# The last expert's kept sums in a fused attention and mixture-of-experts kernel: additions by engines in place of accumulating transfers, a last batch by eight products, and input quarters made earlier

## The chip, the cores and the metric

The kernel runs on one core of one Trainium2 chip. The metric is the device time of one execution in microseconds (us). In the main comparison the four executions of the kernel before lie within 0.3% (832.15 to 834.22 us). The kernel before took a median of 832.4 us in the main comparison. Experiments are compared by their ratio to runs of the kernel before on the same chip. A profiled execution has a span, from the first to the last instruction, that is 1.7 to 1.9 us shorter than its device time.

Engines: PE is TensorE (matrix products), PEld its weight loads, DVE is VectorE, ACT is ScalarE, POOL is GpSimd, SP is SyncE, which here only issues transfers. Sixteen DMA engines move the data. A transfer issued by POOL appears in a software queue (q0) of the profile, one issued by SP or ACT in a hardware queue (q1, q10).

## The reference, cut to what matters

```python
# attention with a hash mask: B, H, S, D = 4, 8, 768, 64; its output becomes x: 3072 tokens x 512
logits = x @ w_gate                      # 8 experts; P: 8 rounds of row and column normalisation
out = np.zeros((N, D), dtype=np.float32)
for e in range(E):                       # w1[e]: 512 x 1024, w2[e]: 1024 x 512
    h = np.maximum(x @ w1[e], 0.0)
    ye = h @ w2[e]
    out += P[:, e:e + 1] * ye
```

Every expert works on every token. The sum over the experts is what the change is about.

## The kernel before

The kernel keeps the whole output, 3072 x 512 in f32, as running sums `acc` in SBUF, and adds each expert to it. For experts 1 to 7 both products use a scheme with seven products of half-size blocks in place of eight, paid for with sums of the blocks ("quarters" of x, w1 and w2, and the half sums `hs` of h). Per expert there are four batches of 768 tokens. While TensorE makes the hidden layer of one batch (`hidden`), it makes the second product of the batch before (`mixed`) in between: `woven` interleaves the two step by step.

One step `i` of `mixed` makes two blocks of 128 tokens. Of its products three are gathered straight into `acc` by VectorE, and four intermediate ones are copied, scaled, to a tile `vt` by ScalarE. The copies are then added to `acc` by an accumulating transfer:

```python
    outv = out.rearrange("(b r j m) d -> b j m r d", b=B, r=R, j=J)
    # ... cut: in mixed(e, b), for each i; vt is [128, 4, 256] f32, 512 KB
            def keep(k, p):
                if last and k == 1:
                    gather(k, a, p)
                    return
                pin(nc.scalar.activation(out=vt[:, k], in_=a, func=Act.Copy, scale=p))
                # ... cut: in the very last step VectorE adds vt[:, k] itself
            # ... cut: the seven products
                if g == 6:
                    if not last:
                        pin(nc.gpsimd.dma_start(out=acc[:, b, i], in_=vt, accum_op=Alu.add))
                    if e == E - 1 and not last:
                        for j in (i, J // 2 + i):
                            pin((nc.gpsimd if final else nc.sync).dma_start(
                                out=outv[b, j], in_=sums_of(b, j).rearrange("p c d -> p (c d)")))
                    next(coming)          # one step of GpSimd's work on the next expert's weights
```

With the last expert each pair of blocks is stored as soon as its transfer has landed: 22 stores of 256 KB, and for the very last pair four of 128 KB. Look at the order in `outv`: for fixed `b, j` a store's target is `m r d`, that is 4 x 32 x 512, because a tile's partition is `m * 32 + r` while neighbouring rows of the output differ in `m`.

The quarters of x are made by VectorE, one batch per round of the weave, in the first three rounds:

```python
        parts = quarters_of_x(n + 1) if n + 1 < B else iter(())
        # ...
            if g in (10, 19, 28, 37):
                next(parts, None)         # one of four VectorE operations, 128 x 768 f16
```

GpSimd makes the quarters of the next expert's weights at the same time, one operation of 128 x 1024 f16 after each accumulating transfer that it issues.

The softmax here doesn't subtract the row's maximum and nothing guards it: scores larger than these inputs give would overflow.

## Time and profile before

| | before |
|---|---|
| time, median of 3 runs | 832.17 us (832.15 to 834.22) |
| span of the profiled execution | 832.5 us |
| TensorE's last product ends | about 791.6 us |
| TensorE busy from 345 to 778 us | 432.66 of 433 us |
| TensorE idle from 270 to 320 us | 5.15 us |

First the page's picture of the span in 40 slices of 20.8 us, busy tenths of TensorE and of the DMA engines, kernel before.

```profile
PE   3979999999899899999999999999999999999800
DMA  6965687531020454666496467648745864456743
```

TensorE works until slice 38 and does nothing in the last two. The DMA engines still do. The second view gives the busy time of each engine by stretch: us of the stretch, then busy us and instructions of each engine, the granted clock of TensorE, the DMA share and GB/s.

```profile
270.00:320.00 50.00, 44.85 (x326) 31.45 (x324) 44.84 (x87) 36.28 (x81) 15.39 (x12) 1.00 0.49 85
320.00:345.00 25.00, 24.45 (x183) 17.66 (x182) 17.70 (x42) 19.86 (x44) 10.61 (x8) 1.00 0.45 86
345.00:778.00 433.00, 432.66 (x3278) 319.94 (x3277) 330.07 (x772) 282.82 (x657) 162.61 (x130) 1.00 0.63 115
```

From 345 us to the tail TensorE is the limit and has no gap worth speaking of. Between 270 and 320 us it idles 50 - 44.85 = 5.15 us.

The chain of waits, kernel before, its end: start in us, duration, what was waited for.

```profile
783.90 10.41 DMA acc<-vt
794.32 1.22 issue
795.53 0.53 POOL out_dram L288
...
796.97 21.15 DMA acc<-vt
818.12 0.28 issue
818.40 0.71 POOL out_dram L288
```

Two accumulating transfers, one after the other, take 31.6 of the last 48.6 us. Over the whole run such a transfer takes a median of 4.9 us. The timeline of the store queue and the DMA queues say why these take longer. The two first lines are issues of single stores by SP, one early and one late; the third, from the table of DMA queues for 794 to 796 us, when only stores were moving, gives packets, MB and share of 16 engines.

```profile
758.41 0.54 SPq L288 DMA_DIRECT2D out_dram<-acc  x1
805.13 5.16 SPq L288 DMA_DIRECT2D out_dram<-acc  x1
q1 hardware_dynamic: 98, 0.20, 26.6%
```

An issue takes 0.54 us when the queue has room and 5.16 us when it must wait for room. Stores alone move 0.20 MB in 2 us, about 100 GB/s, and keep 26.6% of the 16 engines busy: 0.266 x 16 = 4.3, as if four engines were at their limit and twelve had nothing to do. The Trainium skill, "DMA: Bandwidth & Descriptors", section "Why a DMA increments its semaphore by 16 and not by 1", says that a transfer is spread over the largest number of engines, up to 16, that divides the slowest dimension of both sides. Here that is 4, from 4 x 32 x 512 in DRAM.

Last, the timeline of 278 to 291 us, lines of GpSimd's and VectorE's additions alone.

```profile
279.22 2.45 POOL L139 TENSOR_TENSOR s<-t 128x1024 f16<-128x1024 f16 x1
279.38 2.73 DVE L646 TENSOR_TENSOR xT<-xT 128x768 f16<-128x768 f16 x1
...
285.20 0.55 DVE L648 TENSOR_TENSOR xd<-xT 128x768 f16<-128x768 f16 x1
...
287.68 2.97 DVE L650 TENSOR_TENSOR xd<-xT,xd 128x768 f16<-128x768 f16 x1
287.82 2.41 POOL L141 TENSOR_TENSOR t<-t 128x1024 f16<-128x1024 f16 x1
```

An operation of this form on VectorE takes 0.55 us alone. The two here that run beside one of GpSimd take 2.7 and 3.0 us, and they end 0.4 us after GpSimd's. The skill, "SBUF — State Buffer", section "Who interferes with whom", describes a port pair that such two operations share and that one of them holds for the whole instruction.

### The profile page before, as it was taken

How to read it: one execution, taken by the hardware profiler on the slowest of the kernel's cores; microseconds unless marked ns; L12 is line 12 of the kernel's file. 1: busy time of each engine (PE TensorE's matmuls, PEld its weight loads, DVE VectorE, ACT ScalarE, POOL GpSimd, SP SyncE). 2: the span in 40 equal slices, each digit the busy share in tenths (PEclk: the TensorE clock that was granted, in tenths of full speed). 3: DMA queues.
4: the chain of work that ended last, by engine and by line, in shares of the span. 5: the costliest groups of instructions: out<-in, count | busy, mean ns of one | idle time of the engine just before them, and what ended most of it. 6: DMA issues, size and time to landing. Idle time of an engine off the chain costs nothing.

```text
span 832.5 us, 16856 instructions
## 1 busy us (share of the span) xinstructions
PE 755.4 (91%) x6412; PEld 525.8 (63%) x6412; DVE 540.0 (65%) x1213; ACT 515.1 (62%) x1033; POOL 309.2 (37%) x323
## 2 busy tenths in 40 slices
PE   3979999999899899999999999999999999999800
PEld 1546656666555666677777777777777777777600
DVE  3435645654566897777777777777777777777700
ACT  0758767678645767766666666666666666666400
POOL 7655245439000333443353344334534433311110
PEclk9879999999899999999999999999999999999965
DMA  6965687531020454666496467648745864456743
GB/s 168 271 158 154 123 200 182 136 78 29 1 51 2 76 95 83 109 126 122 77 162 118 76 119 135 115 90 144 125 87 101 148 108 89 89 106 138 145 112 83
DMA packets 44912, 94.33 MB, mean 113 GB/s; under 512 B 10848, under 2 KB 24160, under 8 KB 44832
## 3 DMA queue, kind: packets, MB, share of 16 engines
q0 software_dynamic: 30112, 77.88, 48.7%
q1 hardware_dynamic: 13920, 14.77, 6.5%
q8 instruction: 50, 0.82, 0.4%
q10 hardware_dynamic: 800, 0.62, 0.3%
q14 instruction: 30, 0.25, 0.1%
HBM read 53.14 MB, written 7.08 MB: 72 GB/s over the span
## 4 chain that ended last, share of the span: by engine, by line
PE 75%; DMA 10%; ACT 5%; DVE 2%; issue 2%; POOL 2%; SPq 1%; POOLq 0%; ACTq 0%; DVEq 0%
PE a L663 17%; PE a L240 16%; PE d L663 12%; PE y L240 8%; PE st L458 5%; DMA acc<-vt 4%; PE d L240 4%; PE hp L516 4%; PE yp L198 2%; PE num L474 2%; ACT pt L461 2%; DMA qs<-t 2%; PE yp L526 2%; PE hp L306 2%; ACT acc L231 2%
## 5 line engine op out<-in xcount | busy, mean ns | idle before, releaser
L247 ACT ACTIVATE vt<-a,p 128x256 f32<-128x256 f32 x335 | 158.8, 474 | 154.6 <-PE a L240 154.6
L672 DVE CUSTOM_DVE_ANT_0 hT<-d,u 128x384 f16<-128x384 f32 x336 | 185.2, 552 | 98.9 <-ACT u L668 95.8
L285 POOL DMA_DIRECT2D acc<-vt x83 | 71.5, 861 | 324.1 <-ACT vt L247 146.8
L461 ACT ACTIVATE pt<-st 128x768 f16<-128x768 f32 x192 | 147.2, 809 | 71.5 <-PE st L458 50.5
L668 ACT COPY u<-a 128x384 f32<-128x384 f32 x336 | 161.2, 480 | 26.6 <-PE a L663 21.1
L240 PEld LDWEIGHTS <-hT 128*128 128x128 f16 x1344 | 131.0, 97 | 52.5 <-issue 2.2
L240 PE MATMUL a<-t,hs 128*128 128x256 f16 x1008 | 151.2, 272 | 4.4 <-ACT vt L247 3.2
L240 PEld LDWEIGHTS <-hs 128*128 128x128 f16 x1008 | 98.4, 98 | 41.8 <-issue 6.0
L663 PEld LDWEIGHTS <-t 128*128 128x128 f16 x896 | 87.7, 98 | 39.1 <-issue 2.9
L458 PE MATMUL st<-qs,ks 71*128 71x384 f16 x384 | 97.7, 337 | 16.2 <-DMA qs<-ds 11.9
L663 PE MATMUL d<-xd,t 128*128 128x384 f16 x448 | 109.4, 326 | 2.6 <-DVE hT L672 2.6
L663 PE MATMUL a<-xT,s 128*128 128x384 f16 x448 | 109.4, 326 | 0.1
L240 PE MATMUL y<-t,hT 128*128 128x256 f16 x672 | 100.7, 272 | 1.2 <-DVE acc L254 1.0
L254 DVE SCALAR_TENSOR_TENSOR acc<-y,p,acc 128x256 f32<-128x256 f32 x168 | 80.2, 478 | 11.7 <-PE y L240 11.6
L474 PEld LDWEIGHTS <-pt 128*128 128x128 f16 x1152 | 62.5, 99 | 28.2 <-issue 3.4
L663 PEld LDWEIGHTS <-s 128*128 128x128 f16 x672 | 65.5, 97 | 17.6 <-issue 2.3
L474 PE MATMUL num<-va,pt 128*128 128x65 f16 x1152 | 68.4, 196 | 0.6 <-ACT pt L461 0.6
L370 POOL CAST t<-acc 128x768 f16<-128x768 f32 x32 | 26.4, 828 | 89.0 <-DVE acc L369 88.2
L458 PEld LDWEIGHTS <-ks 71*128 71x128 f16 x384 | 33.3, 100 | 37.2 <-issue 14.3
L702 ACT ACTIVATE hT<-a 128x384 f16<-128x384 f32 x112 | 54.1, 483 | 1.8 <-PE a L663 1.7
L663 PE MATMUL a<-xd,s 128*128 128x384 f16 x224 | 54.3, 323 | 0.8 <-ACT u L668 0.6
L663 PE MATMUL a<-xT,t 128*128 128x384 f16 x224 | 54.7, 326 | 0.0
(94 smaller groups left out, 965.5 us busy)
## 6 DMA issues: line engine op xcount, KB each, us to landing
acc<-vt POOLq DMA_DIRECT2D x83, 512.0 KB, 4.9
t<-in_moe_w_dram POOLq DMA_DIRECT2D x24, 512.0 KB, 7.6
acc<-in_k_dram POOLq DMA_DIRECT2D x7, 768.0 KB, 5.8
acc<-in_q_dram POOLq DMA_DIRECT2D x7, 768.0 KB, 6.4
v<-in_v_dram POOLq DMA_DIRECT2D x28, 192.0 KB, 4.7
out_dram<-acc SPq DMA_DIRECT2D x18, 256.0 KB
t<-in_moe_w_dram POOLq DMA_DIRECT2D x4, 1024.0 KB, 10.6
ks<-t SPq DMA_DIRECT2D x64, 48.0 KB
```

The source lines that it names most:

```text
L240: pin(nc.tensor.matmul(dst, hq[hn][:, fo, :], wq[wn][:, fo, :], start=first and fo == 0, stop=fo == FH - 1, skip_group_check=True))
L247: pin(nc.scalar.activation(out=vt[:, k], in_=a, func=Act.Copy, scale=p))
L254: pin(nc.vector.scalar_tensor_tensor(out=dst, in0=src, scalar=p, in1=dst, op0=Alu.mult, op1=Alu.add))
L285: pin(nc.gpsimd.dma_start(out=acc[:, b, i], in_=vt, accum_op=Alu.add))
L458: pin(nc.tensor.matmul(st[:, i, 0:HT], d["k"][0:KR, h, kt * P:(kt + 1) * P], d["q"][0:KR, h, i * HT:(i + 1) * HT], start=True, stop=True))
L461: pin(nc.scalar.activation(out=pt, in_=st[:, :, 0:HT], func=Act.Exp, scale=scale))
L474: pin(nc.tensor.matmul(num[:, j * (D + 1):(j + 1) * (D + 1)], pf[:, j * P:(j + 1) * P], va[:, h, kt, :], start=(kt == 0 and j == 0), stop= ...
L516: pin(nc.tensor.matmul(hp[:, 0:HT], w1[:, do, fo * P:(fo + 1) * P], xT[:, do, b * S + t * HT:b * S + (t + 1) * HT], start=(do == 0), stop= ...
L663: pin(nc.tensor.matmul(bk, wq[wn][:, do, f * P:(f + 1) * P], xq[xn][:, do, :], start=first and do == 0, stop=do == 1, skip_group_check=True))
L668: pin(nc.scalar.copy(t, bk))
L672: pin(add(TENSOR_ADD_SAT, out=dst, in0=bk, in1=u, s0=3e38, s1=0.0))
L702: pin(nc.scalar.activation(out=hT[:, f, hi], in_=a, func=Act.Relu))
```

## The change

Its intent: no accumulating transfer with the last expert, so that the last stores don't wait for one; a last batch whose blocks are finished one after the other; and quarters of x that are all made before the second round.

```diff
@@ mixed
-                    if not last:
+                    if e < E - 1:
                         pin(nc.gpsimd.dma_start(out=acc[:, b, i], in_=vt, accum_op=Alu.add))
-                    if e == E - 1 and not last:
+                    else:
+                        eng = nc.vector if i == J // 2 - 1 else nc.gpsimd
+                        pin(eng.tensor_tensor(acc[:, b, i], acc[:, b, i], vt, op=Alu.add))
                         for j in (i, J // 2 + i):
-                            pin((nc.gpsimd if final else nc.sync).dma_start(
-                                out=outv[b, j], in_=sums_of(b, j).rearrange("p c d -> p (c d)")))
+                            pin(nc.sync.dma_start(out=outv[b, j],
+                                                  in_=sums_of(b, j).rearrange("p c d -> p (c d)")))
@@ new: the last batch of the last expert, by whole products
+    def final():
+        e, b = E - 1, B - 1
+        w2, hT = weights[e, 2], hts[e, b]
+        for j in range(J):
+            yp = (yps if j % 3 < 2 else y2ps).tile([P, DD], F32, tag="y", name="yp")
+            # ... cut: 8 products of 512 columns (the last block in two halves), then
+                pin(nc.vector.scalar_tensor_tensor(out=dst[:, cols], in0=yp[:, cols], scalar=...,
+                                                   in1=dst[:, cols], op0=Alu.mult, op1=Alu.add))
+                pin((nc.sync if cols.start == 0 else nc.scalar).dma_start(out=outv[b, j][:, :, cols],
+                                                                          in_=dst[:, cols]))
@@ woven
-        parts = quarters_of_x(n + 1) if n + 1 < B else iter(())
+        parts = chain(*(quarters_of_x(m) for m in range(1, B))) if n == 0 else iter(())
-            if g in (10, 19, 28, 37):
+            if g % 4 == 2:
                 next(parts, None)
```

Cut: for the last expert one sum of w2's blocks goes to a tile of its own instead of overwriting a quarter of w2, because `final` needs w2 as it was; `quarters_of_x` got a `yield` at its end; the special cases of the very last step fell away.

## The prediction

> **What bounds it now.** Up to 778 us TensorE: the busy table by stretch has it busy 432.7 of 433 us from 345 to 778, at full clock. Two places lose time.
>
> (1) The tail. The last product ends near 791.6 us, the span at 832.5. In between, the chain of waits holds almost only the last accumulating transfers `acc<-vt` (10.4 and 21.2 us; the median is 4.9) and the stores behind them. The store queue's timeline shows issues of 0.55 us until 760, then back-pressure of 4 to 7 us each. By the DMA view, stores alone (794 to 800) take 25.7% of 16 engines, 97 packets of 2 KB per 2 us, 97 GB/s: four busy engines, 85 ns a packet. The Trainium skill, "DMA: Bandwidth & Descriptors", section "Why a DMA increments its semaphore by 16 and not by 1", says a transfer is spread over the largest k up to 16 that divides both sides' slowest dimension; in DRAM the store's is 4 (4x32x512). The trace agrees. The accumulates need the same four engines and crawl.
>
> (2) From 270 to 320 TensorE idles 5.15 of 50 us (0.55 in the next 25). Four VectorE operations that make input quarters took 2.6 to 3.0 us instead of 0.55, each overlapping a 2.4 us GpSimd operation. The skill, "SBUF — State Buffer", section "Who interferes with whom", gives such a pair one exclusive port; the durations agree.
>
> **What changes.** Gone: 11 accumulating transfers, all of the last expert's. New: six GpSimd additions of 128x1024 f32 (estimate 2.4 us, as its f16 operations of 1024 columns), three on VectorE (estimate 1.2 us, from 422 ns at 256 columns). The last batch takes 48 products of 512 columns, 10.3 us, 1.71 a block, in place of 84 of 256 with stalls (13 us). Stores still have four engines. Eight quarter operations move to 250–270 us, where GpSimd does no arithmetic and VectorE is about half busy.
>
> **On the critical path.** Quarters: about 3.3 us back. VectorE's additions: up to 1 us lost. TensorE then ends near 788, and its own tail would end near 793. But stores bound the end: 128 packets on four engines are about 2.62 us a store. The third batch's middle pair, ready at 773, flows from 775 to 780, its last pair to 785.5, the last batch's six (five of 2.62, one in half rows, 3.2) to 802; completion and end add 2. So 804 us: some 3 us from the quarters, 25 from the tail.
>
> **Predicted: 804 us, 8 in 10 between 797 and 812. Faster by over 2%: 0.96; within 2%: 0.03; slower: 0.01.**
>
> **What would show it.**
> - No `acc<-vt` in the last expert; only hardware queues there, at 25% of 16 engines at the end.
> - Store issues of 0.55 us until about 775, back-pressure again for the last batch.
> - The last product ends 10 to 15 us before the last store lands; the chain ends in `out_dram<-acc`, not in TensorE.
> - TensorE's idle time from 270 to 320 falls below 2.5 us; no quarter operation takes over 1 us.
> - VectorE's half sums stay at 415 to 428 ns: GpSimd's additions end before they start.
>
> **What would make it wrong.** Stores on more than four engines: then the end is TensorE's, near 793. GpSimd additions over 4.5 us: they block half sums, and TensorE stalls six times by some us. Stores alone below 97 GB/s: 810 or later. The earlier quarters may delay the routing's VectorE chain at 250 to 256, under 1 us.

## The result, and the profile after

| | before | after |
|---|---|---|
| time, median of 4 runs | 832.44 us | 805.37 us (803.74 to 806.08) |
| ratio | 1 | 0.9668 (95% interval 0.9647 to 0.9688) |
| span of the profiled execution | 832.5 us | 804.0 us |
| VectorE's last operation, on TensorE's last product, ends | 792.2 us | 787.7 us |
| from there to the end of the span | 40.3 us | 16.3 us |
| TensorE idle from 270 to 320 us | 5.15 us | 1.52 us |

A ratio here is the mean time of one kernel's runs over that of the other's in the same rounds, so it is not quite the ratio of the medians.

The 40 slices, kernel after (20.1 us each).

```profile
PE   3969999999999999999999999999999999999991
DMA  6966676641002264486468657745964676541222
```

TensorE now works up to the last slice but one and a little into the last. The DMA share of the last three slices is a steady two tenths. Busy time by stretch, kernel after:

```profile
270.00:320.00 50.00, 48.48 (x358) 34.65 (x356) 35.97 (x85) 39.87 (x89) 17.99 (x14) 1.00 0.51 90
320.00:345.00 25.00, 24.26 (x181) 17.35 (x180) 18.21 (x43) 19.92 (x45) 9.33 (x9) 1.00 0.51 96
```

TensorE's idle time from 270 to 320 us fell from 5.15 to 1.52 us, and VectorE's busy time from 44.84 to 35.97 us. VectorE lost eight operations to an earlier stretch (8 x 0.55 = 4.4 us) and some 9 us that those had taken longer than 0.55 us beside GpSimd; part of the room is filled by other work that now comes sooner.

The chain of waits, kernel after, its end, followed by what SP, which waits for the last stores, waited for (total us, times, longest):

```profile
777.42 8.18 PE yp L304 x41
...
786.16 1.05 PE yp L304 x8
787.21 0.03 issue
787.24 0.48 DVE acc L306
```

```profile
SPq L796 <- DMA out_dram<-acc: 9.0, 5, 2.5
```

The chain view stops at VectorE's last operation at 787.7 us, because it goes back from the last instruction and the landing of a store is none. The 16.3 us that follow are the stores. The lines of the store queue show them: two groups of issues (line 290 is in `mixed`, line 309 in `final`; durations are ns, lowest, median and highest), then the DMA queue between 796 and 800 us.

```profile
L290 SPq DMA_DIRECT2D out_dram<-acc x18: 536/537/633, 727.6 to 777.6; - x18
L309 SPq DMA_DIRECT2D out_dram<-acc x6: 537/1466/4467, 778.7 to 790.1; - x6
q1 hardware_dynamic: 205, 0.41, 26.3%
```

The 18 stores of the first three batches issue without any wait. The six of the last batch come every 1.7 us and are held back up to 4.5 us, and after TensorE has ended, the queue still empties at 0.41 MB in 4 us, again on a quarter of the engines.

What the change added was cheap, as this view of groups by shape shows (line, engine, operation, count, busy us, mean ns):

```profile
L288 POOL TENSOR_TENSOR acc<-acc,vt 128x1024 f32<-128x1024 f32 x6 | 14.1, 2357 | 38.8 <-DVE acc L254 30.4 <-ACT vt L250 8.5
L288 DVE TENSOR_TENSOR acc<-acc,vt 128x1024 f32<-128x1024 f32 x3 | 3.7, 1227 | 0.3
```

### The profile page after: what moved, and what is told of

Same layout as the page of the kernel before. It is cut to its first block, busy times and chain, and to the rows that moved or that the text cites. A ratio compares the mean times of both kernels' runs of the same rounds, so it can differ in the third digit from the quotient of the medians.

```text
span 804.0 us, 16754 instructions
## 1 busy us (share of the span) xinstructions
PE 756.1 (94%) x6384; PEld 523.1 (65%) x6384; DVE 531.0 (66%) x1198; ACT 509.1 (63%) x1022; POOL 310.1 (39%) x314
## 4 chain that ended last, share of the span: by engine, by line
PE 79%; DMA 6%; ACT 5%; DVE 2%; POOL 2%; SPq 2%; issue 2%; POOLq 0%; ACTq 0%; DVEq 0%
PE a L679 18%; PE a L246 17%; PE d L679 13%; PE y L246 8%; PE st L473 5%; PE d L246 4%; PE hp L531 4%; PE yp L206 3%; ACT pt L476 2%; PE num L489 2%; DMA qs<-t 2%; PE hp L321 2%; DMA qs<-ds 1%; PE yp L541 1%; SPq L389 1%
## 5 line engine op out<-in xcount | busy, mean ns | idle before, releaser
L250 ACT ACTIVATE vt<-a,p 128x256 f32<-128x256 f32 x324 | 153.3, 473 | 149.2 <-PE a L246 148.9
L684 ACT COPY u<-a 128x384 f32<-128x384 f32 x336 | 160.9, 479 | 22.4 <-PE a L679 20.1
L285 POOL DMA_DIRECT2D acc<-vt x72 | 61.4, 852 | 267.9 <-ACT vt L250 112.3
L246 PEld LDWEIGHTS <-hT 128*128 128x128 f16 x1296 | 126.3, 97 | 50.7 <-DVE hT L688 1.1
L246 PE MATMUL a<-t,hs 128*128 128x256 f16 x972 | 145.8, 272 | 2.0 <-ACT vt L250 1.5
L246 PEld LDWEIGHTS <-hs 128*128 128x128 f16 x972 | 94.8, 98 | 38.3 <-issue 2.8
L246 PE MATMUL y<-t,hT 128*128 128x256 f16 x648 | 97.1, 272 | 0.0
L254 DVE SCALAR_TENSOR_TENSOR acc<-y,p,acc 128x256 f32<-128x256 f32 x162 | 77.4, 478 | 11.4 <-PE y L246 11.4
L679 PEld LDWEIGHTS <-s 128*128 128x128 f16 x672 | 65.5, 97 | 17.6 <-issue 2.3
L385 POOL CAST t<-acc 128x768 f16<-128x768 f32 x32 | 26.3, 826 | 89.5 <-DVE acc L384 89.3
```

The costliest lines, as they stand in the source:

```text
L246: pin(nc.tensor.matmul(dst, hq[hn][:, fo, :], wq[wn][:, fo, :], start=first and fo == 0, stop=fo == FH - 1, skip_group_check=True))
L254: pin(nc.vector.scalar_tensor_tensor(out=dst, in0=src, scalar=p, in1=dst, op0=Alu.mult, op1=Alu.add))
L679: pin(nc.tensor.matmul(bk, wq[wn][:, do, f * P:(f + 1) * P], xq[xn][:, do, :], start=first and do == 0, stop=do == 1, skip_group_check=True))
L684: pin(nc.scalar.copy(t, bk))
```

## The experiments

The theory to test has two parts. First, stores use four DMA engines of 16; in the kernel before the accumulating transfers need those four as well and crawl, and in the kernel after the stores alone still bound the end. Its rivals: the transfers are slow in themselves; the last batch's product bounds the end; the store rate is one of the queue or of the memory. Second, VectorE's quarter operations cost TensorE time by meeting GpSimd's, not by being there. Its rival: VectorE simply has too much to do in that stretch.

The experiments ran on four chips; runs of one chip share the runs of the kernel before.

| run | what | median, us | ratio to before | 95% interval |
|---|---|---|---|---|
| change | the changed kernel, first comparison | 805.37 | 0.9668 | 0.9647 to 0.9688 |
| e1 | before, earlier quarters alone | 828.51 | 0.9944 | 0.9907 to 0.9982 |
| e2 | before, quarters at other steps | 832.86 | 0.9981 | 0.9945 to 1.0016 |
| e3 | changed, last batch by seven products | 806.84 | 0.9675 | 0.9646 to 0.9705 |
| e4 | changed, transfers kept | 827.83 | 0.9931 | 0.9891 to 0.9970 |
| e5 | changed, tokens reordered so that stores spread | 796.37 | 0.9559 | 0.9530 to 0.9588 |
| e6 | before, tokens reordered | 808.05 | 0.9678 | 0.9649 to 0.9707 |
| e7 | before, quarters at clearer steps | 830.86 | 0.9954 | 0.9924 to 0.9984 |
| e8 | changed, stores split in four | 794.56 | 0.9524 | 0.9495 to 0.9552 |
| e9 | e8 with seven products | 812.14 | 0.9733 | 0.9705 to 0.9762 |
| e10 | changed, again | 804.44 | 0.9638 | 0.9610 to 0.9667 |
| e11 | e8, last stores on two queues | 793.50 | 0.9503 | 0.9472 to 0.9534 |
| e12 | seven products; ScalarE issues half of the very last pair alone | 802.13 | 0.9605 | 0.9575 to 0.9635 |

All were correct. e1 to e4 ran on one chip, e5 and e6 on a second, e7 to e10 on a third, e11 and e12 on a fourth. Which chip the first comparison had is not recorded.

### e1: the earlier quarters alone

```diff
 # on the kernel before
-        parts = quarters_of_x(n + 1) if n + 1 < B else iter(())
+        parts = chain(*(quarters_of_x(m) for m in range(1, B))) if n == 0 else iter(())
-            if g in (10, 19, 28, 37):
+            if g % 4 == 2:
```

> The kernel before with the earlier input quarters alone. Theory (the later quarter operations of VectorE collided with GpSimd's): all twelve later quarter operations take about 0.55 us, TensorE's idle time from 270 to 320 us falls from 5.15 to about 1.5 us, everything after it comes 3 to 3.6 us sooner, tail included, so about 828.8 us. Rival (the gain is swallowed by the store backlog or by the routing chain before 256 us): 831.5 to 832.5 us.

All quarter operations took 0.55 to 0.56 us, and TensorE's idle time from 270 to 320 us was 1.52 us:

```profile
270.00:320.00 50.00, 48.48 (x361) 34.97 (x360) 35.56 (x84) 39.49 (x90) 17.65 (x13) 1.00 0.53 95
```

The ratio 0.9944 is 4.7 us, with an interval of 1.5 to 7.7, and holds the expected 3.6. So the quarters' part of the gain is real, is not swallowed by the routing, and passes through the tail to the end.

### e2 and e7: the quarters in their place, but at other steps

```diff
 # on the kernel before; e2, then e7
-            if g in (10, 19, 28, 37):
+            if g in ((10, 19, 28, 37) if n == 0 else (10, 24, 28, 42)):
+            if g in ((10, 19, 28, 37) if n == 0 else (8, 10, 24, 26)):
```

> The kernel before with the quarters of the third and fourth batch left where they are, but two of each four shifted by five steps of the weave, away from GpSimd's operations. Collision theory: no quarter operation takes over 1 us, TensorE's idle time from 270 to 320 us falls below 2.5 us, about 829 us, nearly as with the earlier quarters. Rival (VectorE has simply too much to do in that stretch, and its work there is unchanged): idle time stays above 4 us, 831.5 to 832.5 us.

> The kernel before with the quarters of the third and fourth batch left in their stretch, in pairs at steps where the trace of before shows no operation of GpSimd (the shift of the run before this one met GpSimd again: 1.76 to 2.73 us). Collision theory: no quarter operation over 0.7 us, TensorE's idle time from 270 to 320 us under 2.5 us although VectorE has the same work there; 828 to 830 us if before is 832.5. Rival (too much VectorE work in that stretch): idle time above 4 us.

Neither run avoided GpSimd altogether, because the operations came at other times than their steps in the weave had let me reckon. Of the eight operations of that stretch four were still slow in e2 (1.76 to 2.73 us) and two in e7 (2.34 and 2.21 us). One of the two in e7 is this pair of lines of its timeline:

```profile
279.40 2.46 POOL L139 TENSOR_TENSOR s<-t 128x1024 f16<-128x1024 f16 x1
279.95 2.34 DVE L648 TENSOR_TENSOR xd<-xT 128x768 f16<-128x768 f16 x1
```

So the expected 0.6 to 0.7 us per operation and an idle time under 2.5 us were missed in both. But the runs form a series with the same eight operations in the same stretch, in the order in which less and less time is lost beside GpSimd. The time lost is the sum of the eight durations less 8 x 0.55:

| | time lost beside GpSimd, us | TensorE idle, 270 to 320 us |
|---|---|---|
| before | 9.0 | 5.15 |
| e2 | 6.7 | 3.04 |
| e7 | 3.4 | 2.80 |
| e1, the eight operations moved away | 0 | 1.52 |

The rival asked for an idle time above 4 us in e2 and in e7, and both are well below. Meeting GpSimd is therefore a cause. That VectorE's load has no part in it is not shown: no run had the eight operations in the stretch without any meeting, their places in the weave changed together with the meetings, and the idle time does not fall in step with the time lost (from e2 to e7 3.3 us less is lost, but only 0.24 us less is idle). On time, e2 is unclear at this resolution (0.9945 to 1.0016), and e7 gained 0.5%.

### e3: the last batch by seven products again

```diff
 # on the changed kernel, in woven
-        if n == len(work):
-            yield from final()
-            return
-        h = hidden(*work[n])
+        h = hidden(*work[n]) if n < len(work) else iter(())
+        elif n == len(work):
+            plan = 21 * "C"
```

> The changed kernel with the last batch by seven mixed products again, its kept sums added by the engines. Theory (stores on four DMA engines bound the end): the last product comes about 3 us later, yet the last store lands within 1.5 us of the changed kernel's, so 803 to 807 us: the eight products are worth nothing while stores bound the end. Rival (TensorE's tail bounds the end, and the eight products were a part of the gain): 808 us or more.

TensorE's last product ended 2.8 us later than in the changed kernel (790.0 against 787.2 us), and an addition by VectorE followed it, the last line of VectorE's timeline, e3:

```profile
790.65 1.23 DVE L288 TENSOR_TENSOR acc<-acc,vt 128x1024 f32<-128x1024 f32 x1
```

VectorE so ended at 791.9 in place of 787.7 us, but the span was 804.9 against 804.0 us and the ratio 0.9675 against 0.9668. In the changed kernel the eight products were worth nothing that can be seen: the stores' end hides them.

### e4: the transfers kept for the first three batches

```diff
 # on the changed kernel, in mixed
-                    if e < E - 1:
-                        pin(nc.gpsimd.dma_start(out=acc[:, b, i], in_=vt, accum_op=Alu.add))
-                    else:
-                        eng = nc.vector if i == J // 2 - 1 else nc.gpsimd
-                        pin(eng.tensor_tensor(acc[:, b, i], acc[:, b, i], vt, op=Alu.add))
+                    pin(nc.gpsimd.dma_start(out=acc[:, b, i], in_=vt, accum_op=Alu.add))
+                    if e == E - 1:
```

> The changed kernel with the last expert's nine accumulating transfers of the first three batches kept, in place of the additions by GpSimd and VectorE; the last batch by eight products. Theory (transfers and stores compete for the same four DMA engines): stores are back-pressured from the first batch on as in the kernel before, and the end comes at 818 to 824 us. Rival (only the transfers of the last batch, which stood in the chain, cost anything): 804 to 807 us.

The span was 823.4 us and the median 827.8 us, some us over the expected range (the kernel before took 834.1 on this chip) and far from the rival's. One sign failed: the stores were not held back from the first batch on. Of the issues up to 760 us none took over 1.1 us; after that single ones took up to 8.2 us. TensorE's last product ended at 784.3 us, and yet the end came 39 us later. The store queue's timeline, e4, its last entry, six stores of the last batch:

```profile
796.24 16.80 SPq L306 DMA_DIRECT2D out_dram<-acc  x6
```

They could not even begin to be issued before 796 us, because the stores of the batches before stood in the queue. So it is not that a transfer stood last in the chain. The last of the nine transfers had been issued at 773.9 us, and its last packet ended at 783.8 us; the transfers had used up time of the four engines in which stores should have run (the packet counts under e6 show this sharing), and the stores that waited for them began later. Against the changed kernel, the additions by GpSimd and VectorE are worth 0.9931 - 0.9668 = 0.0263 of 832 us, about 22 us, nearly the whole change. The two ratios were measured in different comparisons; by their intervals the 22 us are good to about 4.

### e5 and e6: stores that spread over 16 engines, on both kernels

The tokens inside a tile of 128 are put in another order. The transposes of q write with a step, and a store's target becomes 32 x 4 x 512. Bytes and packets stay the same, except that the output's neighbours now lie in neighbouring partitions.

```diff
 # on the changed kernel (e5) and on the kernel before (e6)
-    outv = out.rearrange("(b r j m) d -> b j m r d", b=B, r=R, j=J)
+    outv = out.rearrange("(b r j m) d -> b j r m d", b=B, r=R, j=J)
             else:
-                o_ap = o_ap.rearrange("p (m r) -> p m r", r=R)
+                i_ap = i_ap.rearrange("p (j m) d -> p j m d", m=M4)
+                o_ap = o_ap.rearrange("p (j r m) -> p j m r", j=J, m=M4)
```

> The changed kernel with the tokens inside each 128-row tile ordered so that a store's slowest dimension in DRAM is 32 in place of 4 (the transposes of q write with a stride, the stores read r before m; same bytes, same packets of 2 KB). Theory (each store runs on four of 16 DMA engines): stores now run on 16, issues stay at 0.55 us to the end, the stores land a few us behind TensorE's last product near 787 us, and the time is 791 to 795 us. Rival (the rate of 97 GB/s is one of the store queue or of writes to DRAM in this pattern): the rate stays, 803 to 807 us. If the strided transposes cost VectorE time in the attention part, that shows before 225 us and is to be told apart by the start of the routing.

> The kernel before with the same order of tokens and nothing else. Theory (the accumulating transfers were slow because four engines carried the stores too): the last transfers land in about 5 us in place of 10 and 21, and the end comes 9 to 13 us after the last product at 791.6 us: 801 to 806 us, about as much as the whole change gained. Rival (the transfers are slow in themselves, whatever the stores do): 815 us or more.

The DMA queue of e5 between 780 and 782 us:

```profile
q1 hardware_dynamic: 338, 0.63, 82.2%
```

That is 0.63 MB in 2 us, three times the 0.20 MB of before, on 82% of the engines. So the limit of 100 GB/s was neither one of the queue nor of the memory. The span ended 3.6 us behind VectorE's last operation, in place of 16.3 us. The median of 796.4 us lies just above the expected range: on this chip the kernel before took 834.5 us, and the routing began 2.2 us later than in the changed kernel (229.4 against 227.2 us). The transposes with a step take longer (1.25 us in the median against 0.97, 1.58 at most against 0.98), but how much of the 2.2 us is theirs is open, since in e8, without them, the routing began at 229.8 us.

In e6 the transfers are still there, eleven of them with the last expert. The end of its chain of waits:

```profile
791.50 4.51 DMA acc<-vt
796.01 0.29 issue
...
797.47 4.91 DMA acc<-vt
802.38 1.25 issue
```

The same two transfers that took 10.4 and 21.2 us in the kernel before take 4.5 and 4.9 us. Nothing was changed about them; only the stores were spread.

The packet records of the traces, which `prof` sums but does not list, show the sharing itself (packets of 512 bytes and more). While only stores ran in the kernel before (794.4 to 797.0 us), four packets were under way at a time for 2.13 of the 2.6 us and five for 0.46, never more. In e5, from 780 to 782 us, it was 15 to 17 for 1.33 of the 2 us. While the transfer of 21.2 us ran beside stores in the kernel before (798.0 to 818.1 us), stores and transfer together had four or five packets under way for 12.0 of the 20.1 us. The transfer has 256 packets: 194 had started by 805 us, and the other 62, about a quarter, which would be the part of four engines of 16, trickled out until 817 us. In e6 all 256 started within 5 us. The records don't name the engine of a packet; that the four are the same ones is read from these counts.

From VectorE's last operation (799.8 us in this execution, whose routing began at 235.5 us) to the end it is 8.3 us, in place of 40.3. With a ratio of 0.9678, three new lines about the order of rows, in place of two, gain as much as the whole change, 0.9668. The median is 2 us above the expected range. The profiled execution is the slowest of its five, and the late start of its routing (235.5 us) is more than those 2 us; why it began so late is not settled, and e5 with the same transposes began 6 us earlier.

### e8 and e11: the store split in four, without another order of tokens

A store of 128 partitions becomes four of 32, each 32 x 512 on both sides.

```diff
 # on the changed kernel; used in mixed and in final
+    def store(b, j, cols, both):
+        src = sums_of(b, j).rearrange("p c d -> p (c d)")
+        for m in range(M4):
+            eng = nc.scalar if both and m % 2 else nc.sync
+            pin(eng.dma_start(out=outv[b, j][m][:, cols], in_=src[R * m:R * (m + 1), cols]))
 # in mixed: e8: both = (b == B - 1), which never holds there; e11:
+                            store(b, j, slice(0, DD), b >= B - 2 and i == J // 2 - 1)
 # in final:
+                store(b, j, cols, True)
```

> The changed kernel with each 256 KB store issued as four of 32 partitions each, whose slowest dimension is 32 on both sides (in the last batch in turn on two queues), and the order of tokens as before: no strided transposes. Four-engine theory: stores spread over 16 engines, the end lies 3 to 4 us behind TensorE's last product near 787 us, as with the changed order of tokens but without the 2 us that its transposes cost earlier: a ratio to before of 0.949 to 0.953, near 791 us on a chip where before takes 832.5. Rival (the changed order of tokens helped in another way, such as neighbouring rows in DRAM): 800 us or more.

> The split stores with eight products, and the third batch's last pair of stores also given to two queues in turn, because in the first run of split stores the store queue's last issue came 3.5 us after VectorE's last operation. The best version tried: the last store lands about 4 us after VectorE's last operation in place of 6, so about 2 us less than that run, a ratio to before near 0.950. Rival (the issue queue does not matter at the end): no change, 0.952.

e8 gave 0.9524, within the expected range, and 1.2% less than the changed kernel on the same chip (e10, 0.9638). Its DMA queues between 786 and 788 us, SP's and ScalarE's:

```profile
q1 hardware_dynamic: 199, 0.28, 46.7%
q10 hardware_dynamic: 96, 0.13, 29.9%
```

That is 0.41 MB in 2 us on 77% of the engines. So it is the spread that helps, not the neighbourhood of rows. The 2 us that were to be saved on the transposes did not show: the routing began at 229.8 us here too. In e8 the span ended 5.4 us behind VectorE's last operation, because SP was still issuing stores 3.0 us after it (the 3.5 us and the 6 of the expectation of e11 count from TensorE's last product). In e11, where ScalarE, idle by then, issues half of the third batch's last pair too, it ended 3.4 us behind it (785.0 and 788.4 us). The ratio of 0.9503 is the best of all, but the difference to e8's 0.9524 is inside the intervals, and they ran on two chips; only the shorter tail is shown.

### e9 and e12: seven products once the stores are out of the way

```diff
 # on e8 (e9) and on e11 (e12): the edit of e3; in e12 ScalarE issues only for the very last pair
```

> The same split stores, with the last batch by seven mixed products. With stores out of the way TensorE's tail should count: its last product came 3 us later in the run of seven products, and VectorE adds 1.2 us behind it, so 3 to 5 us more than the split stores with eight products. Rival (the eight products are worth nothing even then): within 1 us of them.

> Seven products in the last batch with split stores, mended: in the first try ScalarE had to issue stores between its own copies and TensorE waited for it. Here it issues only half of the very last pair, after its last copy. If TensorE's tail counts once stores are out of the way, this takes 4 to 6 us more than the run beside it with eight products (last product 3 us later, 1.2 us of VectorE's addition and more issues behind it). Rival (eight products are worth nothing even then): within 1.5 us of it.

e9 took 17.6 us more than e8, far over the expected 3 to 5, and was badly made. In it ScalarE issues stores in the middle of the last batch, and between them it has copies to make for which TensorE waits. Its timeline:

```profile
786.02 1.83 ACTq L136 DMA_DIRECT2D out_dram<-acc  x4
787.90 0.47 ACT L256 ACTIVATE vt<-a,p 128x256 f32<-128x256 f32 x1 [5.25 <-DMA out_dram<-acc]
788.42 1.01 PE L252 MATMUL a<-t,hs 128*128 128x256 f16 x4 [4.18 <-ACT vt L256]
```

ScalarE stood still for 5.25 us because an issue in its queue waited for GpSimd's sum, and TensorE stood still for 4.18 us because of ScalarE. This happened twice. The run says nothing of the eight products, only that an engine whose work is awaited is no place for a store that waits.

e12 is the mended run, and it took 8.6 us more than e11 on the same chip (0.9605 against 0.9503), where 4 to 6 were expected. The profiled executions lie further apart, at spans of 801.0 and 788.4 us, mainly because e11's is the fastest of its six. Of these 12.6 us, 3.5 were there before the last batch began: the last product of the hidden layer ended at 776.2 against 772.7 us, 1.5 us of it from a later start of the routing, the rest in a stretch in which the two kernels are the same. From there to TensorE's last product it took 16.4 us with seven products and 11.8 with eight. What TensorE waited for in e12 from 770 us on (total us, times, longest):

```profile
PE a L252 <- ACT vt L256: 1.8, 3, 0.6
PE d L252 <- DVE hT L692: 1.3, 1, 1.3
PE a L252 <- DVE hs L230: 0.5, 1, 0.5
```

These are 3.6 us, against 1.1 in e11, and the granted clock was 0.66 from 780 to 785 us, against 1.00 in e11. VectorE then added 1.3 us more behind TensorE than in e11, and the stores took 6.6 us behind VectorE in place of 3.4. That last difference need not be the products': e12 gives only half of the very last pair to ScalarE, e11 half of the whole last batch and of the pair before it. So the eight products do count, by several us, but only in a kernel whose stores spread. Which share belongs to the clock and to the way of issuing is open.

### e10: the changed kernel again

> The changed kernel itself, on the same chip as the two runs before it, for comparison: a ratio to before of 0.965 to 0.969, the last store landing some 15 us behind the last product.

0.9638, a little below the expected range, with the last operation of VectorE at 787.6 us and a span of 802.9 us: 15.3 us of stores, as expected.

## Why the prediction was right

The time was predicted as 804 us, with 797 to 812, and measured as 805.37. Point by point:

- **What bounds the kernel before.** Four engines for the stores, transfers that crawl beside them: confirmed by e6, where the same transfers took 4.5 and 4.9 us, by the packets counted there, and by e5, where stores reached 82% of the engines.
- **The stores bound the end.** This is the step on which the forecast rested: a TensorE-bound end would have been near 793 us. It was confirmed by the 16.3 us behind VectorE's last operation and by e3, in which a later last product cost nothing. With the stores spread (e5, e8, e11) the TensorE-bound end appeared: spans of 793.0, 795.2 and 788.4 us.
- **2.62 us a store, the last at 802 us, and 2 us to the end.** Measured: 26.3% of the engines, 0.41 MB in 4 us, which is 2.6 us a store; the queue ran dry just after 802 us, and the span was 804.0 us.
- **The costs of what was added.** GpSimd's addition 2.36 us against an estimate of 2.4; VectorE's 1.23 against 1.2; a block of the last batch 1.73 us against 1.71. The half sums stayed at 414 to 428 ns.
- **The quarters.** About 3.3 us were predicted, and 3.6 us of TensorE's idle time went; no quarter operation took over 0.56 us. e1 alone gained 4.7 us, with an interval that holds both.
- **VectorE's additions, up to 1 us.** A little too small: TensorE idled 0.48 us in each of the two stretches 730 to 750 and 750 to 770, and 0.54 us before the last batch, 1.5 us in all. Nothing of it shows in the time, as the stores bound the end.
- **Signs that were wrong in form.** The chain of waits was to end in `out_dram<-acc`. It ended in VectorE's last operation, since that view follows instructions. And the last product was to end 10 to 15 us before the last store landed; it was 15.3 us or a little more. Back-pressure came in the last batch alone, after 780 us, as forecast.
- **The split of the tail's 25 us.** The prediction gave them to the change of the tail as a whole. e3 and e4 divide them: about 22 us to the additions by engines, nothing visible to the eight products.

## What to carry to other kernels

Before moving work between engines to save a transfer, look at how many DMA engines the transfer's neighbours use: here a share that stood still near 25% while a queue was held back was four engines of 16, and the cure was the slowest dimension of the access pattern, which took three lines and gained as much as the whole change. When a tail moves, ask what becomes its next limit before counting what the new work saves: the eight products were worth nothing behind the stores and several us once the stores were out of the way. And place an operation of VectorE with two inputs in SBUF where GpSimd is not computing, and a waiting store on a queue whose engine nobody waits for.

## What the Trainium skill lacked or had wrong

- "DMA: Bandwidth & Descriptors", section "Why a DMA increments its semaphore by 16 and not by 1": the rule for the number of engines held. What the page does not have is a measured rate of such a store: stores of 256 KB in packets of 2 KB ran at 0.20 MB in 2 us on four engines (26.6%), and at 0.63 MB in 2 us (82.2%) after the slowest dimension went from 4 to 32.
- The same page has no measured figure for how a store on few engines drags other transfers. Two accumulating transfers of 512 KB took 10.4 and 21.2 us beside such stores, and 4.5 and 4.9 us when the stores were spread (e6).
- The same page, section "Issuing engines are not separate DMA queues", speaks of the issuing sequencer's time as usually small. Here an issue took 0.54 us with room in the queue and up to 7.0 us (kernel before) and 8.2 us (e4) without, and in e9 a store waiting in ScalarE's queue stopped its copies for 5.25 us.
- "SBUF — State Buffer", section "Who interferes with whom": agrees that operations of VectorE and GpSimd block each other (0.55 us became 2.6 to 3.0 us). It says that the one that issues first holds the ports. In one case here VectorE's record starts 0.14 us before GpSimd's (287.68 and 287.82 us), and yet VectorE's was the one drawn out to 2.97 us; the start in a record need not be the moment at which the ports are taken, which no run here shows.
- No page that was read gives the price of a 32x32 transpose on VectorE that writes f32 with a step: 128 x 768 took 0.97 us without a step and up to 1.58 us with a step of 16 bytes (e5).
